# Where two small stores stand in a queue of weight loads

## The chip, the cores and the metric

The kernel runs on one core of one Trainium2 chip. The metric is the device time of one execution in microseconds (us). Times below are medians of several executions. Kernels whose ratios come from the same rounds ran in turn on the same chip; the three later sets of rounds ran on three different chips (that of the first isn't on record), and the kernel before took 2845, 2837, 2828 and 2827 us in the four sets. So only kernels of one set are compared closely.

## The reference, cut to what matters

The program computes two unrelated heads and joins them. The second is a long convolution (an S4 layer), which the change doesn't touch. The first is a recurrent attention over 64 segments; each segment needs the memory rows that the segment before has produced.

```python
mem = mem0                                     # 8 memory rows
for s in range(n_seg):                         # 64 segments of 32 rows
    xs = x[:, s * seg_len:(s + 1) * seg_len, :]
    h = jnp.concatenate([mem, xs], axis=1)     # 40 rows of 1024
    q = einsum('btd,dhe->bhte', h, Wq)         # 32 heads of 128
    k = einsum('btd,dhe->bhte', h, Wk)
    v = einsum('btd,dhe->bhte', h, Wv)
    ...                                        # masked softmax attention
    o = einsum('bhte,hed->btd', o, Wo)
    mem = o[:, :M, :]
    outs.append(o[:, M:, :])
```

The four weight matrices are 8 MB each in bf16 and don't fit on the chip together. So most of them stay resident in SBUF, and the rest is streamed from DRAM again in each of the 64 steps.

## The kernel before

A step works in the order k0, q0, k1, q1, v0, v1 (two halves of each projection, 8 tiles of 512 KB to a half), then 16 tiles of the output projection. `STREAM` says which tiles are streamed: 16 per step. They go through four buffers of one pool (`wst`), in turn.

```python
STREAM = {("k", 0): (0, 5), ("q", 0): (3,), ("k", 1): (0, 4), ("q", 1): (0, 4), ("v", 0): (0, 4), ("v", 1): (0, 4)}
STREAM_O = (0, 4, 8, 11, 13)
SLOTS = 4

def unit(key):                                   # the weight tile `key`
    if key in W_res:
        return W_res[key]                        # resident
    if key in kept:
        return ahead_of.pop(key)                 # two tiles are kept in PSUM
    between.pop(key, lambda: None)()             # what is to be issued just ahead of this load
    t_ = wst.tile([128, 2048], BF16, name="wst", tag="w%d" % (loads[0] % SLOTS))
    loads[0] += 1
    nc.sync.dma_start(out=t_[:], in_=WD[key][:])     # L239
    return t_

def stores(s, ob):
    nc.sync.dma_start(out=OLd[s], in_=ob[:, 1, :])   # L302
    nc.sync.dma_start(out=out_a[...], in_=ob[:, 0, :])   # L304
```

All these DMAs are issued by SyncE (SP) in program order. An issue that must wait for something holds up every issue behind it (in the step whose lines the prediction shows, the first k1 load by 3.2 us). The result of a step is the tile `ob`. Its first half is transposed into `hT`, which holds the step's input rows, and only then can the next step's k0 start. Both halves are stored.

```python
for s in range(NS):
    ...
    between["k", 0, 5] = lambda: pks.append(load_pk(s))
    if s:
        between["k", 1, 0] = lambda: stores(s - 1, ob)
    a = quads("k", 0, range(KC))           # matmuls of L317
    k0 = evac(a, "A")
    a = quads("q", 0, range(KC))
    q0 = evac(a, "B")
    ...
    a = quads("k", 1, H0)                  # tiles 0 to 3
    QT0 = new_qt()                         # takes the place of ob (tag "E")
    tr(p0, 1, q0, QT0[:], nc.scalar.copy)  # four transposes
    quads("k", 1, H1, a)                   # tiles 4 to 7
    ...
    oproj(pp[:, 1, :], range(12, 16), o1)  # matmuls of L416
    ob = work.tile([128, 2, 256], BF16, name="ob", tag="E")
    nc.vector.tensor_copy(out=osb[:, 0:128], in_=pp[:, 1, 0:128])
    nc.scalar.copy(out=osb[:, 128:256], in_=pp[:, 1, 128:256])
    ...                                    # transposes of ob into hT, pieces of the next k0
    nc.scalar.copy(out=ob[:, 1, :], in_=pp[:, 0, :])   # L499
```

## Time and profile before

| what | before |
|---|---|
| median of the first three runs | 2844.76 us (2843.34 to 2845.94) |
| span of the profiled run, mean granted TensorE clock | 2845.9 us, 0.894 |
| loop of 64 steps | from about 1,002 to 2,740 us |
| one step (61 whole steps in the trace) | 27.09 us |
| DMA share and rate in the loop | 0.93, 326 GB/s |
| wait of SP's queue for ob, at the first store | 179.4 us over 64 steps |

The prediction below shows the lines and reads them. A line of the waits has who waited, for whom, the total in us, how often, and the longest. A line of the timeline has the start and the duration in us; the duration of a row with "x2" runs from the first of two issues to the end of the second. In the table of stretches each row is a window of time; the last three columns are the granted TensorE clock, the mean busy share of the 16 DMA engines and the rate in GB/s.

### The profile page before, as it was taken

The numbers are of one execution on the slowest core, as the hardware profiler recorded it, in microseconds if no ns is written. First come the engines' busy times: TensorE is split into PE (matmuls) and PEld (weight loads), VectorE is DVE, ScalarE is ACT, GpSimd is POOL, SyncE is SP. The second block draws the span as 40 slices with busy tenths as digits, with TensorE's granted clock in tenths as the row PEclk, the third lists the DMA queues.
The fourth block names the chain that finished last, engine by engine and source line by source line (L and its number), as shares of the span: only waits on it lengthen the run. The fifth ranks groups of instructions, "written<-read, shape, count | busy, mean of one in ns | idle before, by whom it ended". The sixth has DMA issues, their size and how long they took to land.

```text
span 2845.9 us, 76496 instructions
## 1 busy us (share of the span) xinstructions
PE 2139.7 (75%) x32902; PEld 1125.6 (40%) x32902; DVE 1517.2 (53%) x3202; ACT 1016.3 (36%) x1522; POOL 365.3 (13%) x545
## 2 busy tenths in 40 slices
PE   1478777756797478888888888888788887888847
PEld 0245444542243134444444444444344444444423
DVE  7576677765985145454454454544545545445420
ACT  4767688751121123222232232232222322323320
POOL 2253444542000100000000000000000000000000
PEclk8698998977899789998999998999999999999978
DMA  4545655435335889999999998999999999999981
GB/s 111 146 152 161 176 165 140 134 93 163 100 130 190 309 314 325 324 327 316 321 340 334 327 322 315 330 319 334 320 321 324 331 327 328 328 325 342 325 303 36
DMA packets 377508, 734.86 MB, mean 258 GB/s; under 512 B 115958, under 2 KB 208118, under 8 KB 375120
## 3 DMA queue, kind: packets, MB, share of 16 engines
q1 hardware_dynamic: 352866, 679.52, 70.4%
q0 software_dynamic: 8528, 28.41, 2.9%
q10 hardware_dynamic: 15774, 22.03, 2.4%
q8 instruction: 257, 4.21, 0.6%
q14 instruction: 83, 0.68, 0.1%
HBM read 675.04 MB, written 67.37 MB: 261 GB/s over the span
## 4 chain that ended last, share of the span: by engine, by line
DMA 38%; PE 24%; DVE 2%; ACT 1%; issue 1%; SPq 0%; ACTq 0%; DVEq 0%
PE acc L317 15%; DMA wst<-WD_o 15%; DMA wst<-WD_v 9%; DMA wst<-WD_k 7%; DMA wst<-WD_q 4%; PE pp L416 3%; PE pe L526 2%; DMA olr<-OLd 1%; PE tr L328 1%; ACT ev L323 1%; DVE ob L491 1%; PE pv L385 1%; ACT ob L492 1%; PE tro L496 1%; DVE piece L261 0%
## 5 line engine op out<-in xcount | busy, mean ns | idle before, releaser
L317 PEld LDWEIGHTS <-hT 128*32 128x32 bf16 x12352 | 344.7, 103 | 511.1 <-issue 271.8
L317 PE MATMUL acc<-wst,hT 128*32 128x512 bf16 x2816 | 306.3, 420 | 183.1 <-DMA wst<-WD_k 89.9
L323 ACT CAST ev<-acc 128x512 bf16<-128x512 f32 x384 | 225.1, 586 | 518.6 <-PE acc L317 517.6
L416 PEld LDWEIGHTS <-oT 128*32 128x32 bf16 x8192 | 209.1, 98 | 201.0 <-issue 174.2
L317 PE MATMUL acc<-W_k,hT 128*32 128x512 bf16 x2816 | 249.3, 459 | 0.0
L317 PE MATMUL acc<-W_q,hT 128*32 128x512 bf16 x3328 | 242.8, 399 | 0.0
L416 PE MATMUL pp<-wst,oT 128*32 128x256 bf16 x2560 | 132.2, 283 | 127.5 <-DMA wst<-WD_o 118.4
L261 DVE TENSOR_SCALAR piece<-keep 128x256 int32<-128x256 int32 (+1 forms) x640 | 189.9, 361 | 62.4 <-PE pp L416 57.6
L416 PE MATMUL pp<-W_o,oT 128*32 128x256 bf16 x5120 | 214.7, 278 | 0.0
L317 PE MATMUL acc<-W_v,hT 128*32 128x512 bf16 x3072 | 210.9, 379 | 0.0
L355 DVE TENSOR_REDUCE mx<-sc 128x8 f32<-128x320 f32 x128 | 62.9, 491 | 237.7 <-PE sc L348 237.2
L329 DVE COPY KT<-tr 128x512 bf16<-128x512 bf16 x64 | 27.2, 425 | 273.3 <-PE tr L328 273.3
L336 POOL COPY KT<-pk 128x128 bf16<-128x128 bf16 x128 | 37.9, 296 | 905.5 <-PE acc L317 558.9
L403 ACT CAST oT<-pv 128x512 bf16<-128x512 f32 x128 | 75.0, 586 | 182.5 <-PE pv L389 182.0
L1001 PE MATMUL hps<-KT,MF 128*128 128x512 bf16 x384 | 103.2, 419 | 47.5 <-DVE x L1012 24.2
L1083 PE MATMUL yp<-Bt,mi 128*128 128x512 bf16 x384 | 114.6, 405 | 32.1 <-DVE Bt L1037 16.2
L329 ACT COPY QT<-tr 128x512 bf16<-128x512 bf16 x128 | 75.0, 586 | 141.9 <-PE tr L328 141.0
L295 POOL COPY hT<-xt 128x192 bf16<-128x192 bf16 x64 | 22.4, 349 | 789.7 <-DMA xt<-XTd 531.7
L492 ACT CAST ob<-pp 128x128 bf16<-128x128 f32 x64 | 17.0, 266 | 291.0 <-DVE ob L491 291.0
L130 PE MATMUL pro<-xTl,wsl 128*128 128x512 bf16 x512 | 114.7, 380 | 7.2 <-DVE ua L790 4.6
L885 DVE SCALAR_TENSOR_TENSOR nr<-kM,ptt 128x656 f32<-128x656 f32 x128 | 106.0, 828 | 23.0 <-ACT kM L884 22.8
L491 DVE CAST ob<-pp 128x128 bf16<-128x128 f32 x64 | 18.6, 291 | 180.5 <-PE pp L416 180.5
(266 smaller groups left out, 3861.7 us busy)
## 6 DMA issues: line engine op xcount, KB each, us to landing
wst<-WD_o SPq DMA_DIRECT2D x320, 512.0 KB
wst<-WD_k SPq DMA_DIRECT2D x256, 512.0 KB
wst<-WD_v SPq DMA_DIRECT2D x256, 512.0 KB
wst<-WD_q SPq DMA_DIRECT2D x192, 512.0 KB
Ud<-ux POOLq DMA_DIRECT2D x16, 1024.0 KB, 5.2
uq<-Ud SPq DMA_DIRECT2D x32, 512.0 KB
pk<-PKd SPq DMA_DIRECT2D x64, 192.0 KB
wsl<-in_A_Wk_dram SPq DMA_DIRECT2D x16, 512.0 KB
```

The lines of the kernel that those rows point to most:

```text
L130: nc.tensor.matmul(a[:], lhsT=w[:, kc, 128 * j:128 * j + 128], rhs=xTl[:, kc, :, :].rearrange("p s k -> p (s k)"), start=(kc == 0), stop=( ...
L261: nc.vector.tensor_scalar(out=out.bitcast(I32), in0=in_.bitcast(I32), scalar1=0, scalar2=None, op0=ALU.bitwise_or)
L317: nc.tensor.matmul(a[32 * g:32 * g + 32, o_:o_ + rhs.shape[1]], lhsT=hT[:, kc, :], rhs=rhs, start=(kc == 0), stop=(kc == KC - 1), tile_pos ...
L323: nc.scalar.copy(out=q[:], in_=a[:])
L329: eng(out=dst, in_=p[:, i, :, :, :])
L355: nc.vector.tensor_reduce(out=mx[:], in_=sc, axis=AX.X, op=ALU.max)
L403: nc.scalar.copy(out=o[:], in_=p[:].rearrange("p a (g q) -> p a g q", g=4))
L416: nc.tensor.matmul(po[32 * qt:32 * qt + 32, :], lhsT=oT[:, h % 4, (h % 16) // 4, :], rhs=columns(w, 1024 * hh + 256 * qt, 256)[0][1], star ...
L526: nc.tensor.matmul(pe[b][n][:], lhsT=ol[b][:, hi, :, :].rearrange("p s k -> p (s k)"), rhs=wos[u][:, 1024 * hh + 512 * n:1024 * hh + 512 * ...
L885: v.scalar_tensor_tensor(out=nrs[e // 4][:, e % 4].rearrange("p f t j -> p f (t j)"), in0=kM[:], scalar=MAGIC, in1=ptv, op0=ALU.subtract, ...
L1001: pe.matmul(ps[:], lhsT=MF[:, 4 * rr + mc, cs, 128 * kc:128 * kc + 128], rhs=rhs, start=(i == 0 and mc == 0), stop=(i == 1 and mc == 3))
L1083: pe.matmul(yp[:], lhsT=m_[:, cs, kc, :], rhs=Bt[:, kc, half, j, c_, :], start=(n == 0), stop=(n == 15))
```

## The change

The intent is to let the next step's loads pass the two stores in SP's queue.

```diff
-STREAM = {..., ("k", 1): (0, 4), ...}
+STREAM = {..., ("k", 1): (0, 3), ...}
...
         between["k", 0, 5] = lambda: pks.append(load_pk(s))
         if s:
-            between["k", 1, 0] = lambda: stores(s - 1, ob)
+            between["k", 1, 3] = lambda: stores(s - 1, ob)
```

The first part serves the second. The stores hang on the load of a streamed tile, and they must stand in the program before `QT0` takes ob's place, which is after tile 3 of k1. So tile 3 is streamed in place of tile 4.

## The prediction

> **What bounds the kernel now.** I read the page first: the slices, then the chain that ended last. The kernel has two parts. For some 1,000 us it prepares (the second head, and transposes and projections for the first); then a loop of 64 steps, from about 1,002 to 2,740 us, runs the recurrent attention. The change touches the loop alone.
>
> ```profile
> PE   1478777756797478888888888888788887888847
> ...
> DMA  4545655435335889999999998999999999999981
> GB/s 111 146 152 161 176 165 140 134 93 163 100 130 190 309 314 325 324 327 316 321 340 334 327 322 315 330 319 334 320 321 324 331 327 328 328 325 342 325 303 36
> ...
> DMA 38%; PE 24%; DVE 2%; ACT 1%; issue 1%; SPq 0%; ACTq 0%; DVEq 0%
> ```
>
> From slice 15 on the DMA engines are 9 tenths busy or more and move 315 to 340 GB/s, and the chain is DMA more often than PE. So the loop is paced by streaming weights: in each step 16 tiles of 512 KB come from DRAM into 4 buffers (two each for k0, k1, q1, v0, v1, one for q0, five for the output projection), beside two small loads (pk, 192 KB; xt, 48 KB) and two stores of 64 KB each from the tile ob. All are issued by one queue, SP's, in program order. A load is issued when the tile four loads earlier has been used.
>
> What the change concerns shows in the waits of SP's own queue, taken over the loop:
>
> ```profile
> SPq L239 <- PE acc L317: 399.4, 574, 2.1
> SPq L302 <- ACT ob L499: 179.4, 64, 7.3
> ```
>
> The first row is the normal wait: a load (L239) waits for a buffer. The second is the one to see: the first store (L302) stands at the head of the queue until ACT has written ob, 179.4 / 64 = 2.80 us per step. The next load, k1 tile 0, stands behind it, although its buffer is that of the output projection's tile 13, which PE has used before the last two tiles, the casts and ob.
>
> One step in the timeline, of SP and then of PE, where it hurts:
>
> ```profile
> 1845.22 0.32 SPq L239 DMA_DIRECT2D wst<-WD_q  x1
> 1850.67 0.32 SPq L302 DMA_DIRECT2D OLd<-ob  x1
> 1851.09 0.56 SPq L304 DMA_DIRECT2D out_dram<-ob  x1
> 1851.74 1.72 SPq L239 DMA_DIRECT2D wst<-WD_k  x2
> ```
>
> ```profile
> 1848.02 0.62 PE L416 MATMUL pp<-wst,oT 128*32 128x256 bf16 x8 [2.62 <-DMA wst<-WD_o]
> ...
> 1857.95 0.40 PE L317 MATMUL acc<-wst,hT 128*32 128x512 bf16 x4 [0.33 <-DMA wst<-WD_k]
> ```
>
> PE is through with tile 13 by about 1848.5 (8 matmuls that start at 1848.02), yet k1 tile 0 is issued only at 1851.74, 3.2 us later. What the DMA engines do meanwhile, in the table of stretches (last two columns: DMA share, GB/s):
>
> ```profile
> 1845.20:1849.20 4.00, 1.38 (x32) 0.85 (x23) 0.00 (x0) 0.00 (x0) 0.00 (x0) 0.73 1.00 396
> 1849.20:1852.70 3.50, 2.65 (x30) 1.04 (x26) 1.87 (x7) 0.64 (x2) 0.00 (x0) 0.50 0.27 95
> 1852.70:1856.70 4.00, 4.00 (x69) 1.90 (x65) 0.35 (x1) 1.17 (x2) 0.30 (x1) 0.85 0.88 264
> ```
>
> They run dry: 396 GB/s before, 95 GB/s for 3.5 us, and back only after the load is issued. That step is a bad one. To size the hole for all steps I took every eighth step and the 3.5 us from its OLd store on, and as a last row 61 whole steps:
>
> ```profile
> 1116.22:1119.72 3.50, 3.18 (x32) 1.51 (x36) 1.58 (x6) 0.00 (x0) 0.00 (x0) 0.55 0.73 235
> 1335.23:1338.73 3.50, 3.17 (x36) 1.45 (x38) 1.58 (x6) 0.00 (x0) 0.00 (x0) 0.54 0.61 188
> 1549.15:1552.65 3.50, 3.19 (x58) 1.76 (x62) 1.58 (x6) 0.59 (x1) 0.30 (x1) 1.00 0.90 310
> 1767.44:1770.94 3.50, 3.17 (x33) 1.42 (x36) 1.58 (x6) 0.00 (x0) 0.00 (x0) 0.50 0.55 169
> 1983.37:1986.87 3.50, 3.19 (x33) 1.50 (x37) 1.58 (x6) 0.00 (x0) 0.00 (x0) 0.53 0.89 268
> 2202.22:2205.72 3.50, 3.17 (x37) 1.46 (x40) 1.58 (x6) 0.00 (x0) 0.00 (x0) 0.54 0.50 138
> 2416.89:2420.39 3.50, 1.35 (x24) 0.68 (x28) 1.58 (x6) 0.00 (x0) 0.00 (x0) 1.00 0.97 312
> 2630.45:2633.95 3.50, 2.63 (x49) 1.48 (x53) 1.58 (x6) 0.38 (x1) 0.30 (x1) 1.00 0.87 298
> 1060.73:2713.15 1652.42, 1354.19 (x25986) 693.36 (x25986) 795.74 (x2196) 471.93 (x915) 57.47 (x183) 0.93 0.93 326
> ```
>
> A step takes 1652.42 / 61 = 27.09 us and moves 326 x 27.09 = 8,831 KB. The eight stretches average 240 GB/s, 840 KB in 3.5 us; so the other 23.59 us run at (8,831 - 840) / 23.59 = 339 GB/s. At that rate the 840 KB would take 2.48 us. The hole is worth 3.5 - 2.48 = 1.02 us per step, very uneven: 0.3 us in the best of the eight steps, 2.1 us in the worst.
>
> **What the Trainium skill says.** "DMA: Bandwidth & Descriptors", section "Anatomy of one DMA", says that DMA engines don't wait on semaphores; the wait is on the issuing sequencer, before dispatch. The trace agrees: the 2.80 us per step are SP's, and everything behind in program order waits too. The same page, "Queues, rings and completion order", says that a ring's descriptors are consumed in order, so the stores will now move behind the k1 load; the views I read don't separate the rings, so this is not shown. Its "Specifications" give a ceiling of 435 GB/s; the best stretch here has 396 over 4 us, so the 339 between holes includes pauses that are not of this queue order. "TensorE: Matmul & The Clock Gate", section "What's actually happening", says that PE drops to half clock after an idle window of about 3.4 us and recovers after a busy one. The trace has clock 0.50 to 0.55 in five of the eight stretches: k0 and q0 often run at half speed, which delays the release of the buffers that refill the queue.
>
> **The change part by part.** Nothing is added or removed: by the instruction order each engine has the same work as before. (1) The two stores move from ahead of k1 tile 0 to behind it, ahead of the next streamed tile. Only one load passes them inside the loop: the words of the change say two, but the compiled order is k0, pk, k0, q0, k1 tile 0, the stores, the second k1 tile. (2) That second k1 tile is now number 3, not number 4; tile 4 becomes resident. Same bytes and same preparation, but PE needs the streamed tile one resident tile and four transposes sooner.
>
> For (1): k1 tile 0 is issued as soon as PE has used tile 13, between 2.5 and 3.2 us sooner (2.5 in the step whose tile 13 starts at 2007.59 and whose k1 load is issued at 2010.53). Its 512 KB are 524 / 339 = 1.55 us of work for the engines, in the queue before they run dry. From issue to moving data took some 1.2 us above (1851.74 to 1852.9 or so), so in bad steps part of the hole stays. I cap what one step can win at 1.3 us: the eight holes 1.07, 1.56, 0.30, 1.75, 0.73, 2.07, 0.28, 0.42 become 1.07, 1.3, 0.30, 1.3, 0.73, 1.3, 0.28, 0.42, mean 0.84 us. I take off 0.1 us because stores in small packets won't move at 339 GB/s wherever they stand (a guess): 0.74 us.
>
> How much of it stays? From there on the engines are ahead by 0.74 us, but each later load still waits for PE to free a buffer. q1 tile 0 needs k0's second buffer and q1 tile 4 needs q0's, and neither is freed sooner, since k0 starts from hT and so from ob. The DMA backlog there is about one load, with less margin than before, least in the half-clock steps. I keep 80%: 0.59 us x 63 steps = 37 us off the path that sets the end.
>
> For (2): before, PE had 12 resident matmuls and four transposes between k1's two streamed tiles (2016.23 to 2017.54 in the timeline, 1.3 us from start to start); after, 8 resident matmuls and no transposes (16 matmuls take 1.05 us in the chain, so 12 some 0.75 us). The second lands one load plus two stores later, some 1.9 us. But PE now finds tile 0 landed early, so it meets tile 3 close to its landing: cost 0 to 0.4 us of PE's time, off the path, because PE waits for loads 117.3 + 48.7 + 42.9 + 19.0 = 227.9 us in the loop (its waits for o, k, v and q tiles), 3.6 us per step. Sum: 2844.8 - 37 = 2808 us.
>
> **The rivals.** Bandwidth alone: the bytes are the same and the engines are 93% busy, so the hole merely moves to the next place where the buffers are all taken. For it: only four buffers, and dips elsewhere in the step. Against: 339 GB/s holds between holes and 396 is reached. It makes 2835 to 2845. Everything is won: hole and startup both vanish and no new one comes, 1.02 us x 63 = 64 us, 2780, faster by 2.3%. For it: PE has 3.6 us of slack. Against: the margin at q1. A new wait: the stores end later by one load, and the tile QT that takes ob's place waits for them, or PE waits for tile 3 with an empty pipeline. Each would show as 0.5 us per step, 30 us back, 2840 or worse. Against: QT is written some 6 us or more after the stores' issue (its copy at 2017.69, the OLd issue at 2009.47).
>
> **Range and chances.** Between the rival of nothing (2840) and all (2780) I put 2808, with 8 in 10 for 2785 to 2834. Faster by over 2% means under 2788, which needs 0.90 us per step, nearly the whole hole: 0.13. Slower by 2% needs a new wait of nearly 1 us per step in place of the old one: 0.02. Within 2%: 0.85.
>
> **What would show it.** In the profile after: SP's wait for ob should shrink from 2.80 us per step to about 1.3, as k1 tile 0 is issued within it; the 3.5 us from the OLd store should move about 300 GB/s with a share near 0.9, and the whole loop 333 instead of 326; PE's wait for k tiles should fall from 48.7 us; a step should last 26.5 us. I am wrong if those stretches fill but the rest of the step falls below 339 GB/s (the hole moved), or if PE or ACT waits for the second k1 tile or for the stores.

## The result, and the profile after

The changed kernel took 2803.61 us (median of 6 runs, 2786.44 to 2810.46). The kernel before took 2845.35 us in the same rounds (2843.34 to 2856.89). The ratio is 0.984, with a 95% interval from 0.9805 to 0.9875. The output is correct. Two more sets of rounds, on two chips, gave 0.9865 (0.9839 to 0.9891) and 0.9907 (0.9879 to 0.9935). By the mean times of the three sets the changed kernel is 45.6, 39.1 and 25.4 us faster, 37 us on average.

The page of the changed kernel, its rate by slice and the head of the chain that ended last:

```profile
GB/s 113 141 133 180 171 172 136 131 96 171 100 103 137 291 333 330 340 348 335 344 333 341 345 351 348 328 339 349 320 344 353 329 343 319 321 335 344 324 314 35
...
DMA 36%; PE 24%; DVE 2%; ACT 1%; issue 1%; SPq 0%; ACTq 0%; DVEq 0%
```

DMA still leads the chain, and most slices of the loop stand above those of before. The waits of SP's own queue in the loop:

```profile
SPq L239 <- PE acc L317: 414.6, 509, 2.7
...
SPq L286 <- PE pp L389: 80.6, 63, 1.9
SPq L302 <- ACT ob L499: 77.8, 64, 7.6
...
SPq L291 <- PE pv L389: 48.5, 57, 1.0
```

The wait for ob at the first store fell from 179.4 to 77.8 us, from 2.80 to 1.22 us per step. It is not gone, because the stores still wait for the same event. But one load now stands ahead of them. SP's timeline in one step shows it:

```profile
1842.11 0.32 SPq L239 DMA_DIRECT2D wst<-WD_q  x1
1843.47 0.32 SPq L239 DMA_DIRECT2D wst<-WD_k  x1
1844.91 0.32 SPq L302 DMA_DIRECT2D OLd<-ob  x1
1845.28 0.55 SPq L304 DMA_DIRECT2D out_dram<-ob  x1
1845.93 0.42 SPq L239 DMA_DIRECT2D wst<-WD_k  x1
```

The first k1 load is issued 1.44 us before the OLd store; before the change it came about 1.1 us after it (1851.74 against 1850.67). So it is 2.5 us sooner; on average over the loop it was 1.07 us after the store and is 1.52 us before it. The same eight steps as in the prediction, 3.5 us from the OLd store on, and 61 whole steps in the last row:

```profile
1121.35:1124.85 3.50, 3.18 (x61) 1.90 (x65) 1.58 (x6) 0.59 (x1) 0.30 (x1) 1.00 0.97 360
1330.02:1333.52 3.50, 3.15 (x33) 1.45 (x36) 1.58 (x6) 0.00 (x0) 0.00 (x0) 0.50 0.87 265
1536.49:1539.99 3.50, 2.91 (x53) 1.66 (x57) 1.58 (x6) 0.59 (x1) 0.30 (x1) 1.00 1.05 404
1739.48:1742.98 3.50, 2.78 (x28) 1.28 (x32) 1.58 (x6) 0.00 (x0) 0.00 (x0) 0.56 1.02 397
1948.42:1951.92 3.50, 3.17 (x38) 1.58 (x41) 1.58 (x6) 0.00 (x0) 0.00 (x0) 0.55 1.02 379
2156.44:2159.94 3.50, 2.33 (x41) 1.28 (x45) 1.58 (x6) 0.09 (x1) 0.01 (x1) 1.00 0.95 339
2370.74:2374.24 3.50, 3.17 (x33) 1.42 (x36) 1.58 (x6) 0.00 (x0) 0.00 (x0) 0.50 0.83 267
2582.54:2586.04 3.50, 3.19 (x33) 1.69 (x37) 1.58 (x6) 0.00 (x0) 0.00 (x0) 0.57 1.02 386
1068.17:2663.74 1595.57, 1329.30 (x25987) 687.81 (x25986) 794.23 (x2196) 471.94 (x915) 57.39 (x183) 0.94 0.96 337
```

The hole is gone. The eight stretches average 350 GB/s, where it was 240, and the worst has 265, where it was 138. Eight steps are a fair sample here: over all 62 inner steps, worked out from the packets' times, the 3.5 us move 352 GB/s, where it was 243. A step takes 1595.57 / 61 = 26.16 us in this trace, 0.93 us less. The accounts close: the stretches move 384 KB more each, which at 339 GB/s is 1.13 us won. The rest of the step moves (337 x 26.16 - 350 x 3.5) / 22.66 = 335 GB/s, where it was 339, which over its 7,591 KB is 0.27 us lost. That leaves 0.86 us, and 0.93 was measured, the difference being rounding of the rates. The profiled run was one of the faster ones (2796 us).

Where the 0.27 us went shows when the busy share of the DMA engines is averaged over some 60 steps by the distance from the end of the step. I worked this out from the packets' times in the traces. Each column is 1 us, and 0 is 0.65 us after the end of the first cast of ob, which is on average the place of the OLd store's issue in both kernels. The last two rows are experiments that are told below.

```
us from the store        -3  -2  -1   0   1   2   3   4   5   6   7   8   9
before                   99  99  95  83  56  80  97  91  94  96  98  98  95
changed                 100  99  99  98  99  98 100  91  98  87  95  92  95
changed, third set      100  99  98  97  97  97  99  92  94  85  91  89  95
stores one load earlier  99  88  61  32  24  79  99  93  97 100 100 100  97
changed, PE kept warm    99  99  98  97  98  99 100  98  96  97  98  97  97
```

The change fills the columns 0 to 2 and opens smaller dips in columns 6 to 8.

### The profile page after: what moved, and what is told of

The parts are those of the page before. It is cut to its first block, busy times and chain, and to the rows that moved or that the text cites. A ratio compares the mean times of both kernels' runs of the same rounds, so it can differ in the third digit from the quotient of the medians.

```text
span 2794.3 us, 76496 instructions
## 1 busy us (share of the span) xinstructions
PE 2113.8 (76%) x32902; PEld 1121.9 (40%) x32902; DVE 1516.4 (54%) x3202; ACT 1016.7 (36%) x1522; POOL 363.0 (13%) x545
## 4 chain that ended last, share of the span: by engine, by line
DMA 36%; PE 24%; DVE 2%; ACT 1%; issue 1%; SPq 0%; ACTq 0%; DVEq 0%
PE acc L317 15%; DMA wst<-WD_o 15%; DMA wst<-WD_k 9%; DMA wst<-WD_v 8%; PE pp L416 3%; DMA wst<-WD_q 2%; PE pe L526 2%; DMA olr<-OLd 1%; PE tr L328 1%; PE pv L385 1%; DVE piece L261 1%; DVE ob L491 1%; ACT ev L323 0%; ACT ob L492 0%; PE tro L496 0%
## 5 line engine op out<-in xcount | busy, mean ns | idle before, releaser
L317 PE MATMUL acc<-wst,hT 128*32 128x512 bf16 x2816 | 300.2, 410 | 159.3 <-DMA wst<-WD_k 85.8
L317 PE MATMUL acc<-W_k,hT 128*32 128x512 bf16 x2816 | 238.6, 442 | 0.0
L329 DVE COPY KT<-tr 128x512 bf16<-128x512 bf16 x64 | 27.2, 425 | 266.1 <-PE tr L328 266.1
L1001 PE MATMUL hps<-KT,MF 128*128 128x512 bf16 x384 | 97.0, 400 | 53.2 <-DVE x L1012 29.7
L881 ACT ACTIVATE E<-pa 128x656 bf16<-128x656 f32 x128 | 91.9, 718 | 52.5 <-PE pa L865 49.0
```

The source lines that it names most:

```text
L317: nc.tensor.matmul(a[32 * g:32 * g + 32, o_:o_ + rhs.shape[1]], lhsT=hT[:, kc, :], rhs=rhs, start=(kc == 0), stop=(kc == KC - 1), tile_pos ...
L329: eng(out=dst, in_=p[:, i, :, :, :])
L881: sc.activation(out=Es[e // 4][:, e % 4], in_=pa[:, :, 0:8 * NJ].rearrange("p f (t j) -> p f t j", t=8), func=ACT.Exp)
L1001: pe.matmul(ps[:], lhsT=MF[:, 4 * rr + mc, cs, 128 * kc:128 * kc + 128], rhs=rhs, start=(i == 0 and mc == 0), stop=(i == 1 and mc == 3))
```

## The experiments

The theory: the store's wait for ob at the head of SP's queue holds back the first k1 load, whose buffer is long free, and the DMA engines run dry behind it. The rivals: the other part of the change (tile 3 for tile 4) pays, because its buffer is released before the four transposes; or the stores' small packets pay, by running later behind a full queue; or holes only move, because bandwidth or the number of buffers sets the pace.

### One part alone

The first kernel has only the new tile; the stores stay where they were.

```diff
-("k", 1): (0, 4)
+("k", 1): (0, 3)
```

> Only the second part of the change: the second streamed tile of k1 is number 3 instead of 4; the stores stay ahead of k1 tile 0. If the head-of-queue wait for ob is the whole cause, nothing is won: ratio to the kernel before 0.995 to 1.005, the 3.5 us from the OLd store still at about 240 GB/s. If the earlier release of that tile's buffer (before the four transposes) is what pays, most of the 1.6% shows here: 0.985 to 0.99.

It took 2847.15 us against 2836.9 us of the kernel before; the ratio is 1.0032 (0.9994 to 1.0071). So the tile alone wins nothing. Its eight stretches average 281 GB/s, above the 240 of the first trace that was expected (over all 62 inner steps 265 against 243, and the wait for ob fell to 154.0 us), but that bought no time. Over 61 steps its rate is 328 GB/s with a DMA share of 0.93, hardly above the 326 of before:

```profile
1070.40:2714.16 1643.76, 1342.18 (x25986) 688.87 (x25986) 793.21 (x2196) 471.95 (x915) 57.46 (x183) 0.94 0.93 328
```

The second kernel has only the new order. The stores are issued right after the load of k1 tile 0, and tile 4 is still the streamed one.

```diff
+        behind.pop(key, lambda: None)()          # in unit(), after the load
...
-            between["k", 1, 0] = lambda: stores(s - 1, ob)
+            behind["k", 1, 0] = lambda: stores(s - 1, ob)
```

> Only the first part: the stores go behind k1 tile 0, and the streamed tiles stay 0 and 4. Head-of-queue theory: the whole gain, ratio 0.98 to 0.988, the hole filled (over 320 GB/s in the 3.5 us). Theory of the tile: ratio near 1, though the queue's wait for ob shrinks all the same.

It took 2801.75 us; the ratio is 0.9881 (0.9846 to 0.9915), 35 us by the means. The eight stretches average 342 GB/s, and the wait for ob fell to 76.0 us. Its wait (line numbers are one higher here) and its 61 steps:

```profile
SPq L303 <- ACT ob L500: 76.0, 64, 7.0
```

```profile
1069.98:2667.90 1597.92, 1336.72 (x25987) 690.13 (x25986) 795.21 (x2196) 471.95 (x915) 57.48 (x183) 0.94 0.95 337
```

The ratio is just outside the range that was written down, but inside the spread of the changed kernel over its three sets (0.984 to 0.9907). The order alone explains the gain; the tile is not shown to add to it.

### More and less of the cost

Here the stores go one load further forward, ahead of q0's tile, so that two loads stand behind the wait.

```diff
-            between["k", 1, 0] = lambda: stores(s - 1, ob)
+            between["q", 0, 3] = lambda: stores(s - 1, ob)
```

> The dose the other way: the stores one load further forward than before, ahead of q0's tile, so that two loads stand behind the wait for ob. Head-of-queue theory: the hole grows by about one load, 1.2 to 1.6 us per step, 75 to 100 us: ratio 1.026 to 1.036. If DMA bandwidth alone sets the pace and holes only move, ratio under 1.01.

It took 2893.68 us; the ratio is 1.0197 (1.0165 to 1.0228), 55 us slower. The wait for ob, in SP's queue:

```profile
SPq L302 <- ACT ob L499: 240.3, 60, 5.5
```

The eight stretches fall to 174 GB/s, and the table above shows the share at 32 and 24 in columns 0 and 1. So the hole grows with the number of loads held back, as the theory says, and the sign and order of size are right. The size was missed: the deficit of the columns -2 to 2 grows by about 1.3 us, which over 63 steps is 82 us, but only 55 us were lost. A part is given back later: columns 6 to 8 are at 100, and over columns 3 to 9 the share is above that of before by 0.17 us per step in sum, 11 of the 27 us. That PE has caught up in the meantime and has freed the buffers would explain it, but this was not tested, and the rest is not located.

Here the stores go one load further back than in the changed kernel, behind both streamed tiles of k1:

```diff
-            between["k", 1, 3] = lambda: stores(s - 1, ob)
+            behind["k", 1, 3] = lambda: stores(s - 1, ob)
```

> The stores one load further back than in the changed kernel, behind both streamed tiles of k1. Head-of-queue theory: the changed kernel's hole is already filled, so within 0.3% of it: ratio 0.981 to 0.987; the wait for ob at the store all but vanishes (under 10 us of the loop). If the wait that is left costs something still, up to 0.5% more is won. If late stores cost through the tile QT that takes ob's place (it waits until they have landed), it is slower than the changed kernel: 0.987 to 1.0, with ACT waiting for a DMA before QT.

It took 2794.22 us (its line numbers are one higher, L303 for the first store); the ratio is 0.9865 (0.9833 to 0.9897), which can't be told from the order alone in the same rounds (0.9881). The wait for ob is gone from SP's queue (6.2 us, once). So what the changed kernel still waits for ob costs nothing that these runs resolve. One of the rivals shows for the first time, small, in ACT's waits:

```profile
ACT QT L330 <- DMA out_dram<-ob: 14.9, 8, 2.3
```

The copy into QT, which takes ob's place, waited in eight steps for the store to land. In the changed kernel this wait doesn't appear.

### The stores on another queue

If only the wait at the head matters, the stores can leave SP's queue altogether. They are issued in the program right after ob is written, from GpSimd's queue in one kernel and from ACT's in the other.

```diff
-        nc.sync.dma_start(out=OLd[s], in_=ob[:, 1, :])
+        nc.gpsimd.dma_start(out=OLd[s], in_=ob[:, 1, :])      # nc.scalar in the other
...                                                            # the second store likewise
-        if s:
-            between["k", 1, 0] = lambda: stores(s - 1, ob)
...
         nc.scalar.copy(out=ob[:, 1, :], in_=pp[:, 0, :])
+        if s + 1 < NS:
+            stores(s, ob)
```

> Order of the loads and streamed tiles as before, but the two stores are issued from GpSimd's queue, right after ob is written, so nothing stands behind them. If the wait of SP's queue is the cause, as much is won as by the change: ratio 0.98 to 0.99, though the stores now reach the DMA engines early and mix with the loads. If what pays is that the stores' small packets run later and are hidden behind a full queue, little is won: over 0.993.

> The same with the stores issued from ACT's queue, which has just written ob and so waits for almost nothing. Queue theory: as the one from GpSimd's queue, 0.98 to 0.99; up to 0.3% worse if the issue time of two DMAs (about 0.9 us) delays ACT's copy of k0. Theory of hidden packets: over 0.993.

From GpSimd's queue it took 2793.09 us, ratio 0.9898 (0.986 to 0.9936); from ACT's 2802.65 us, ratio 0.9923 (0.9893 to 0.9954). The changed kernel ran in the same rounds:

> The changed kernel again, on the chip of these runs, to compare with: ratio 0.981 to 0.988.

It took 2787.18 us, ratio 0.9865 (0.9839 to 0.9891). The first is within its range, the second 0.2% above 0.99; up to 0.3% had been allowed for a delayed copy of k0, which was not looked for. So most of the gain comes without any load passing the stores in a queue, which refutes the theory of the packets as the main cause: here they are issued as soon as ob is written, among the loads. By the means the two kernels are 0.3% and 0.5% slower than the changed one. A candidate for that is the wait of QT in the kernel with GpSimd's queue, which the profile has, and which the changed kernel lacks:

```profile
ACT QT L329 <- DMA out_dram<-ob: 37.0, 18, 3.7
```

But the same wait is 24.9 us in the kernel with ACT's queue, which is the slower of the two, and 45.5 us, in 21 steps, in the last kernel of the next section, which is as fast as the changed one. So by itself it doesn't explain the difference, and no run takes it away. The intervals of the kernel with GpSimd's queue and of the changed one overlap; those of the kernel with ACT's queue (from 0.9893) and of the changed one (to 0.9891) just don't. The cause of the difference stays open.

### Other waits at the head of the queue

SP's queue still waits at its head for the buffers of pk and xt, 80.6 and 48.5 us. In this kernel these two loads are issued by GpSimd:

```diff
-        nc.sync.dma_start(out=pk[:], in_=PKd[j])
+        nc.gpsimd.dma_start(out=pk[:], in_=PKd[j])
...
-        nc.sync.dma_start(out=xt[:].rearrange("p k r -> p (k r)"), in_=XTd[j])
+        nc.gpsimd.dma_start(out=xt[:].rearrange("p k r -> p (k r)"), in_=XTd[j])
```

> The changed kernel with the two small loads, pk and xt, issued from GpSimd's queue: in the changed kernel SP's queue still waits at its head for their buffers, 80.6 us (pk) and 48.5 us (xt) of the loop, about 2.0 us per step, with loads of weights behind them. If every head-of-queue wait starves the DMA engines, some 0.3 to 0.5 us per step is won beside the changed kernel: 0.7 to 1.2% better. If a wait only costs where the engines run dry behind it (the DMA share stays at 0.9 or more around these two), the two waits vanish from the list and the time stays within 0.4% of the changed kernel.

It took 2792.28 us, ratio 0.9881 (0.9847 to 0.9915). The changed kernel, a third time and in the same rounds:

> The changed kernel once more, on the chip of these runs, to compare with: ratio 0.982 to 0.989.

It took 2800.12 us, ratio 0.9907 (0.9879 to 0.9935), a little outside its range. Both waits are gone from the list of the new kernel, and it is 0.3% faster by the means, which the intervals don't tell from nothing. So 2 us of waiting per step at the head of the same queue are worth at most a little, where the 1.6 us by which the change shortens the wait for ob went with 1.3%. The length of a wait doesn't tell its cost. What differs is what the DMA engines do meanwhile: in the first trace of the changed kernel their share, averaged by 1 us, stays between 90 and 100 from 3 us before the issue of pk to 6 us after it, and between 86 and 98 around that of xt, where in the kernel before it fell to 55 behind the issue of the stores.

The last kernel of this kind is the one before, with both stores, pk and xt all on GpSimd's queue, so that SP issues weights alone:

```diff
-        between["k", 0, 5] = lambda: pks.append(load_pk(s))
-        if s:
-            between["k", 1, 0] = lambda: stores(s - 1, ob)
+        between["k", 0, 5] = lambda: (pks.append(load_pk(s)), s and stores(s - 1, ob))
...                       # nc.sync becomes nc.gpsimd for pk, xt and both stores
```

> The kernel before with all small transfers (pk, xt, both stores) on GpSimd's queue, so that SP's queue has only weights. Waits at the head for other things are then zero. Theory as it stands (only the wait for ob starved the engines): as the changed kernel or up to 0.4% worse, since the stores run at once and pk no longer comes in its place: ratio 0.984 to 0.992. If the other waits matter too, better than the changed kernel by 0.5% or more.

It took 2791.94 us, ratio 0.9898 (0.9864 to 0.9932), 0.1% from the changed kernel of these rounds. A queue without any foreign wait is no better than the changed one.

### The dips that opened

Two kernels look for the cause of the dips in columns 6 to 8. The first lets q0 stream its tile 0 in place of 3, so that its buffer is used and released sooner:

```diff
-("q", 0): (3,)
+("q", 0): (0,)
```

> The changed kernel with q0's streamed tile 0 instead of 3: its buffer is released three tiles (about 0.9 us) sooner, so the load of q1's second tile is issued sooner. In the changed kernel the DMA share dips 6 to 7 us after the OLd store, just when that load is awaited. If what limits the gain now is the late release of buffers in k0 and q0, that dip fills and 0.2 to 0.5 us per step is won beside the changed kernel (0.5 to 1.1%). If the dips are not of this load, or PE now waits for the earlier tile as long as it wins, within 0.3% of the changed kernel.

It took 2798.05 us, ratio 0.991 (0.9876 to 0.9943), by the means 0.5% slower than the changed kernel of the same rounds, 0.2% more than either branch allowed. In its trace the second load of q1 is issued only about 0.4 us sooner than in the first trace of the changed kernel (4.12 us after the OLd store on average, against 4.50), not 0.9, and the share in columns 6 to 8 stays at 89, 94 and 91. So this edit doesn't fill the dips. As it brought the load only half as far forward as intended, and as its profiled run was the slowest of the six (2818.86 us), it doesn't refute the idea that buffers are released too late.

The second keeps PE busy with five matmuls per step that compute nothing, three while it would wait for the output projection's tile 13 and two while ob is cast. They write a bank that is free there.

```diff
-        oproj(pp[:, 1, :], range(12, 16), o1)
+        oproj(pp[:, 1, :], range(12, 13), o1)
+        wm = ps_acc.tile([128, 512], F32, name="warm", tag="acc")
+        def warm(n):
+            for _ in range(n):
+                nc.tensor.matmul(wm[:, 0:384], lhsT=ident[:], rhs=ident[:].unsqueeze(1).to_broadcast([128, 3, 128]), start=True, stop=True, skip_group_check=True)
+        warm(3)
+        oproj(pp[:, 1, :], range(13, 16), o1)
...
+            warm(2)                              # before the transposes of ob
```

> The changed kernel with five idle matmuls of 384 columns per step (three between the output projection's tiles 12 and 13, two while ob is cast), into a bank that is free there. In the profiled run of the changed kernel steps with a half-clock stretch took 26.6 us, steps without 25.6. If the half clock eats a part of the gain, fewer such stretches (under 100 us of the loop instead of about 170) and up to 0.5 us per step won, 1%. If the long steps cause the half clock rather than the other way round, or the idle matmuls come in the way, 0 to 1% slower than the changed kernel.

It took 2768.04 us, ratio 0.9815 (0.9782 to 0.9849) to the kernel before, and by the means 0.9904 to the changed kernel of the same rounds. It is the fastest kernel of this study. The stretch of 61 steps:

```profile
1058.31:2635.58 1577.27, 1333.06 (x26291) 690.74 (x26291) 793.81 (x2196) 471.33 (x915) 57.08 (x183) 0.99 0.96 341
```

A step takes 25.86 us, the mean granted clock in the loop is 0.99 where the changed kernel has 0.94, and the rate is 341 GB/s. Summed from the clock's records over the 61 steps, 24 us are at half clock, where the three traces of the changed kernel have 177, 195 and 185 and the kernel before 238. The dips of columns 6 to 8 are gone (97, 98, 97 in the table above). The idle matmuls could act in some other way than by the clock, and a kernel with the same matmuls where PE is busy anyway, as a control, was not run. But the traces without them show the same link. Here the steps of one trace are split by PE's mean clock from 1 us before column 0 to 6 us after it; it is over 0.95 (full) or under 0.8 (half) in all but one of the steps. The loads are given by their issue, in us after the start of column 0, averaged over all steps of a row but at most one.

```
                        steps   share, columns 6-8   q1's second load   v0's first load   step, us
changed, full clock        28                   98               3.79              5.37      25.92
changed, half clock        34                   85               5.02              6.56      26.32
before, full clock         19                  100               3.77              6.22      27.24
before, half clock         42                   97               4.98              6.60      26.97
```

So in the changed kernel the dips are those of the half-clock steps, in which PE releases buffers later and these loads are issued 1.2 us later; the third set's trace has shares of 97 and 82. In the kernel before, q1's load comes as late, yet the share hardly falls and the half-clock steps are no longer than the others. That fits a half clock that became a limit only when the hole in front of it was filled. The step times scatter too much to size it: the difference of 0.40 us has a standard error of 0.27 (in the other two traces of the changed kernel it is 0.18 and 0.40), and the idle matmuls won 27 us, 0.4 us per step.

## Why the prediction was right

The predicted time was 2808 us, and 2803.61 us was measured. The mechanism was that of the prediction, and the experiments of one part alone and of more and less of the cost show it. By its own steps:

- **What moves.** One load passes the stores, 2.5 us sooner, as predicted. SP's wait for ob was to be about 1.3 us per step and is 1.22 us.
- **What is filled: too small.** The prediction filled 0.74 us of a hole of 1.02 us, capping the bad steps at 1.3 us and taking 0.1 us off for slow packets. In the trace the stretches fill completely, to 350 GB/s where about 300 was expected, worth 1.13 us. The cap wasn't needed: even the worst of the eight steps has 265 GB/s. The guess about slow packets wasn't needed either.
- **How much stays: too large.** The prediction kept 80%. In the profiled pair 0.93 of 1.13 us stay, 82%. But the means of the three sets win 0.72, 0.62 and 0.40 us per step (45.6, 39.1 and 25.4 us over 63 steps), which is 64, 55 and 36% of 1.13. So two terms were missed in opposite directions, and the product, 0.59 us, lies in the middle of the three sets. The closeness of 2808 to the measured time is partly luck.
- **What takes the rest back.** The prediction named q1's buffers, which are freed no sooner, and the half clock that makes it worse. Both are in the split of the steps by clock (q1's second load 1.2 us later, share 85 in place of 98), and with the matmuls that keep PE warm the dips close and another 1% is won.
- **The new tile.** It was to cost nothing on the path, and alone it gave 1.0032, within noise of 1. PE's wait for k tiles was to fall from 48.7 us and fell only to 45.2: told apart by tile in the traces, the waits for k1's tile 0 fell from 21.0 to 1.2 us, but those for its second tile rose from 17.8 to 27.2 and those for k0's second from 7.4 to 15.2.
- **The rivals.** That nothing is won is refuted. That everything is won, 64 us, was not reached: the best of the three sets won 45.6. The wait of QT doesn't occur in the changed kernel; it occurs with the stores one load later (15 us) and on other queues (25 to 46 us).
- **Its signs of being wrong.** Both showed, in small. The rest of the step fell from 339 to 335 GB/s, so a quarter of the hole moved (0.27 of 1.13 us), and PE waits for k1's second tile 27.2 us in the loop, 0.4 us per step. Neither outweighs what was won.

What stays open: why the gain differs between the sets, 0.93 to 1.6%. The single runs of one kernel spread by 24 us, and the half-clock stretches differ from trace to trace, but no run separates the two. Whether idle matmuls would help the kernel before was not run; that its half-clock steps are not seen to be longer speaks against it.

## What to carry to other kernels

In a queue that issues in program order, look for a store that waits for the end of a step and stands ahead of loads whose buffers are already free, and let the loads that can be issued pass it. Judge such a wait by what the DMA engines do behind it, in windows of a few us, not by its length. When a hole at one place is filled, look at once for what sets the pace next; here it was PE at half clock, and a few idle matmuls in its waits won about as much again in the same rounds (27 us, after the change's 25).

## What the Trainium skill lacked or had wrong

- "DMA: Bandwidth & Descriptors", section "Issuing engines are not separate DMA queues", says that issuing from several engines at once only saves the sequencer's time to initiate a DMA. Here the two issues take about 0.9 us of SP per step (0.32 and 0.55 us), but what mattered was the wait ahead of them, 2.80 us per step: with the stores issued from GpSimd or ACT, the kernel was 1.0 and 0.8% faster (ratios 0.9898 and 0.9923). The section lacks that a wait ahead of one DMA holds up those behind it on the same engine; it can only be inferred from the page's sentence, which the prediction cites, that the wait is on the issuing sequencer. "Perfetto Trace Analysis", section "DMA Optimizations", does advise one issuing engine for loads and another for stores, but without this reason or a number.
- "TensorE: Matmul & The Clock Gate", section "HAM oscillation — how this bites in real kernels", gives as the rule to have no idle gaps of PE over some 3.4 us, and counts the half clock as a loss of PE's own time. In 61 steps of the kernel before, the longest idle time of PE in the profile is 2.6 us, and there are still 47 half-clock stretches, 238 us in sum. What the trace shows instead is the share of a window: the stretches begin on a grid of 3.41 us, and each of the 46 drops inside these steps follows a window in which PE was busy for 57% or less; 350 windows with more kept the full clock, and so did 17 with 45 to 57%. The page has the window, and a case of short idle times in its next section, but no such share.
- The same page lacks what a half clock costs others. PE is not the bound here, yet in the changed kernel it releases the buffers of a DMA-bound loop 1.2 us later in half-clock steps, and 24 us at half clock in place of 185 in the same rounds went with a ratio of 0.9904.
